# Attention and channel mix on one core: from the ninth head on, ScalarE writes the negated row maxima as diagonal blocks

## The chip, the core and the metric

The kernel runs on one core of a Trainium2 chip. Such a core has a matrix engine (TensorE, in the profile PE for matmuls and PEld for weight loads), VectorE (DVE), ScalarE (ACT), GpSimd (POOL), a queue engine that issues transfers (SyncE, SP) and 16 DMA engines. The metric is the device time of one execution in microseconds (us), as the median of several runs. A profiled execution gives the trace from which all durations below are read.

## The reference

Eight batches of eight heads: the queries are averaged in pairs (1152 to 576 rows per head), then softmax attention over 1152 keys, then a channel mix over the 512 joined features.

```python
def _attn_ref(q, k, v):
    q_pool = q.reshape(B, H, S // 2, 2, D).mean(axis=3)
    scores = scale * np.matmul(q_pool, k.transpose(0, 1, 3, 2))
    scores = scores - np.max(scores, axis=-1, keepdims=True)
    attn = np.exp(scores)
    attn = attn / (np.sum(attn, axis=-1, keepdims=True) + 1e-09)
    return np.matmul(attn, v)

def _moe_ref(x, mu_k, mu_r, w_k, w_v, w_r):
    x_prev = np.concatenate([np.zeros((B, 1, D), dtype=np.float32), x[:, :-1, :]], axis=1)
    xk = mu_k * x + (1.0 - mu_k) * x_prev
    xr = mu_r * x + (1.0 - mu_r) * x_prev
    k = np.maximum(xk @ w_k, 0.0)
    v = k * k @ w_v
    return v / (1.0 + np.exp(-(xr @ w_r)))
```

All inputs are 32-bit floats; the kernel splits each into a 16-bit high part and a 16-bit remainder and adds up the products that matter.

## The kernel before

The 64 heads are worked off one after the other, each in six blocks of 96 queries, 384 blocks in all. For one block, keys lie on the partitions: nine matmuls of 128 keys by 96 queries (line 479) put the high part of the scores into one of three PSUM buffers `s`, which rotate from block to block. The maximum over keys is found in two steps: VectorE reduces the nine chunks (line 486, tile `mx`), a matmul with the identity turns the result (line 489), VectorE reduces it to one maximum per query (line 492, tile `mb`). Then the maxima, which lie one per partition, must come to lie along a row. A matmul with `mb` as a broadcast weight and `negi`, a diagonal of -1/64, as moving operand does this (line 494, called the spread below): it leaves the negated maxima of the 96 queries on every partition of the spare columns of `s`. ScalarE copies one row of it, one partition by 96 elements, into row 96 of the low part of the transposed queries, `qT` (line 497; Prelu with two slopes makes the subtracted value a little larger than the maximum). The nine matmuls of line 503 multiply the second key operand `ks2` with that low part: rows 0 to 63 are the key's high part against the query's remainder, and row 96 of `ks2` holds 64 where the other rows from 64 on hold zero, so the same matmuls subtract the maximum. ScalarE takes the exponential (line 509), GpSimd makes its remainder (line 512), and the matmuls of lines 538, 540 and 545 multiply with the values. Every 256 rows of finished output a channel-mix tile follows (line 684, the largest part of the matmuls), whose ScalarE and VectorE work stands in lines 653 to 748.

No engine chooses its order at run time. Every operation is entered in a list with an engine, an assumed duration, the buffers it reads and writes and a due time. A planner plays the list through with these durations, tries a few orders and writes the best one out; each engine then works through its own list in that order, waiting where an operand is not there. The assumed duration of line 497 is 0.133 us. The change alters the list, so the planner makes a new order for all engines.

Of the kernel before, what the change touches and what calls it, by code (L numbers as in the profile page):

```python
# [11 lines left out]
F32 = mybir.dt.float32  # L12
F16 = mybir.dt.float16
# [3 lines left out]
AF = mybir.ActivationFunctionType  # L17
ALU = mybir.AluOpType
AX = mybir.AxisListType
PSUM = bass.MemoryType.PSUM  # L20
P = 128
# [7 lines left out]
SM = 64.0  # L29
# [8 lines left out]
EPS = 2.0 ** -10  # L38
# [4 lines left out]
O_MAX, O_EXP, O_REST, O_AV, O_EVAC, O_TURN = -6.0, 0.0, 3.0, 14.0, 6.0, 4.0  # L43
# [215 lines left out]
def kernel(  # L259
# [12 lines left out]
    nc = tc.nc  # L272
    B, H, S, D = q.shape
# [6 lines left out]
    QN = 96  # L280
# [4 lines left out]
    HALF = P // 2  # L285
    WIN = [(0, HALF, 0), (HALF, P, 1), (HALF + P, P, 3), (HALF + 2 * P, P, 4), (HALF + 3 * P, P, 5)]
    NW = len(WIN)
    TURN = [(0, 3), (3, 5)]
    assert D == 64 and DM == NG * P and TQ == NB * QN == WIN[-1][0] + P

    def spans(k0, k1):

        return WIN[k0][0], WIN[k1 - 1][0] + WIN[k1 - 1][1]

    const = ctx.enter_context(tc.tile_pool(name="const", bufs=1))
    psum = ctx.enter_context(tc.tile_pool(name="psum", bufs=1, space=PSUM))
    iss = Issue()
    op = iss.add

    def bufs(name, n, shape, dt):  # L300
        return [const.tile(shape, dt, name=f"{name}{i}") for i in range(n)]
# [8 lines left out]
    def half(x, dt, t):  # L310

        return x.bitcast(dt).rearrange("p c (q t) -> p c q t", t=2)[:, :, :, t]


    ident = const.tile([P, P], F32, name="ident")
# [2 lines left out]
    nc.gpsimd.tensor_copy(identb, ident)  # L318
    negi = const.tile([P, P], F16, name="negi")
    nc.gpsimd.tensor_scalar(negi, ident, -1.0 / SM, 1.0, op0=ALU.mult, op1=ALU.mult)  # L320


    kr, vr = bufs("kr", 2, [P, NC, D], F32), bufs("vr", 2, [P, NC, D], F32)
# [11 lines left out]
    cross = const.tile([P, D + 1], F32, name="cross")  # L335
    pl = const.tile([P, NC, TQ], F16, name="pl")
    mx, mb = bufs("mx", 3, [P, QN], F16), bufs("mb", 3, [P, 1], F16)
    den, xb = bufs("den", 2, [P, NW], F32), bufs("xb", 1, [P, NW, 2, D], F32)
    xt = bufs("xt", 3, [P, NG, TQ + 1], F32)
    xm = {n: const.tile([P, NG, T], F32, name=f"x{n}") for n in "kr"}  # L340
# [30 lines left out]

    nc.gpsimd.memset(qn[0][:, 1, :, D:P], 0.0)
    for t_ in ks2:
        nc.vector.memset(t_[D:P], 0.0)
        nc.vector.memset(t_[QN:QN + 1], SM)
    for t_ in vt:
        nc.vector.memset(t_[:, :, 2 * D:2 * D + 2], 1.0)
    for t_ in vb:
# [80 lines left out]
    def block(n, j, i, t):  # L459

        hp, z = n % 2, i % 3
        qi = n // 2 % 2
        q0 = hp * TQ + j * QN
        qhi, qlo = (qT[qi][:, r].rearrange("p j x -> p (j x)")[:, q0:q0 + QN] for r in (0, 1))
        kh, kl = ([(t_, qi, hp, j, j0) for j0, j1 in ((0, 5), (5, NQ)) if q0 < j1 * P and q0 + QN > j0 * P]
                  for t_ in ("qT", "qTl"))
        s = s_b[z]
        rows = slice(j * QN, (j + 1) * QN)
        mxz, mbz = mx[z], mb[z]

        def cols(c0, c1):
            return s[:, P + c0 * QN:P + c1 * QN]

        def grid(c0, c1):
            return cols(c0, c1).rearrange("p (c q) -> p c q", q=QN)

        def scores(c0, c1):
            for c in range(c0, c1):
                nc.tensor.matmul(cols(c, c + 1), ks1[hp][:, c, :], qhi,  # L479
                                 start=(c == c0), stop=False, skip_group_check=True)  # L480

        for c0, c1 in BK:
            op("PE", (c1 - c0) * 0.043, lambda c0=c0, c1=c1: scores(c0, c1),
               r=[("ks1", hp, c) for c in (0, 5) if c < c1 and (c0 < 5 or c)] + kh, w=[("s", z)], key=t)

        op("DVE", 0.967, lambda: nc.vector.tensor_reduce(mxz, grid(0, NC).rearrange("p c q -> p q c"),  # L486
                                                         axis=AX.X, op=ALU.max),
           r=[("s", z)], w=[("mx", z)], key=t)
        op("PE", 0.054, lambda: nc.tensor.matmul(s[0:QN, 0:P], mxz, identb, start=False, stop=False,  # L489
                                                 skip_group_check=True),  # L490
           r=[("mx", z)], w=[("s", z)], key=t + O_MAX)
        op("DVE", 0.199, lambda: nc.vector.tensor_reduce(mbz[0:QN], s[0:QN, 0:P], axis=AX.X, op=ALU.max),  # L492
           r=[("s", z)], w=[("mb", z)], key=t + O_MAX)
        op("PE", 0.05, lambda: nc.tensor.matmul(s[:, 0:QN], mbz[0:QN].broadcast_to([QN, P]),  # L494
                                                 negi[0:QN, 0:QN], start=False, stop=False, skip_group_check=True),
           r=[("mb", z)], w=[("s", z)], key=t + O_MAX)
        op("ACT", 0.133, lambda: nc.scalar.activation(qlo[QN:QN + 1], s[QN:QN + 1, 0:QN], AF.Prelu,  # L497
                                                      scale=1.0 - EPS, alpha=(1.0 + EPS) / (1.0 - EPS)),
           r=[("s", z)] + kl, w=kl, key=t + O_MAX)

        def scores2(c0, c1):
            for c in range(c0, c1):
                nc.tensor.matmul(cols(c, c + 1), ks2[hp][:, c, :], qlo,  # L503
                                 start=False, stop=True, skip_group_check=True)

        for c0, c1 in BK:
            op("PE", (c1 - c0) * 0.043, lambda c0=c0, c1=c1: scores2(c0, c1),
               r=[("ks2", hp)] + kl, w=[("s", z)], key=t + O_EXP)
        op("ACT", NC * QN / 1200 + 0.051, lambda: nc.scalar.activation(  # L509
            pf[:, :, HALF + rows.start:HALF + rows.stop], grid(0, NC), AF.Exp, bias=SHIFT, scale=0.125 / (2.0 * SQ)), r=[("s", z)], w=[("pf", j)], key=t + O_EXP)  # L510
        def lows(to, r0, r1, buf):
            op("POOL", NC * (r1 - r0) / 1000 + 0.066, lambda: nc.gpsimd.tensor_scalar(  # L512
                to, half(pf, U16, 0)[:, :, HALF + r0:HALF + r1], LO, 1.0, op0=ALU.mult, op1=ALU.mult),
               r=[("pf", j)], w=[buf], key=t + O_REST)

        r0 = rows.start
        if j == 0:
            lows(half(pf, F16, 1)[:, :, 0:HALF], 0, HALF, ("pside",))
            r0 = HALF
        lows(pl[:, :, r0:rows.stop], r0, rows.stop, ("pl", j))  # L520

    def window(n, w, t):
# [29 lines left out]
        for c0, c1 in () if side else ((0, 5), (5, NC)):  # L552
            op("PE", (c1 - c0) * 0.030, lambda c0=c0, c1=c1: lo(c0, c1),
               r=[("vb", jv)] + [("pl", j) for j in js] + [("a",)], w=[("a",)], key=t)
        if w < NW - 1:
            return

        u = a_b[:, 0:NW * VN].rearrange("p (k x) -> p k x", k=NW)
        z = n % 2
# [8 lines left out]
        op("DVE", 0.08, lambda: nc.vector.reciprocal(dz, dz), r=[("den", z)], w=[("den", z)], key=t + O_EVAC)  # L568
        op("DVE", 0.07 + NW * D / 960, lambda: nc.vector.tensor_tensor(
            xz[:, :, hh], u[:, :, 0:D], dz.unsqueeze(2).broadcast_to([P, NW, D]), op=ALU.mult),  # L570
           r=[("den", z), ("a",)], w=[("xb", hh)], key=t + O_EVAC)
        if hh == 0:
            return
        for k0, k1 in TURN:
            q0, qe = spans(k0, k1)
# [53 lines left out]
    def turn(n, m=2):  # L629
        cnt[n] += 1  # L630
        return cnt[n] % m
# [7 lines left out]
    def mix(w, t0, t1, key, dk):  # L639
# [4 lines left out]
        for c in range(NG):  # L644
            t = t0
            while t < t1:
# [3 lines left out]
                z = turn("tmp")  # L650
                xk = [("xt", b % 3, c, k0) for k0, k1 in TURN
                      if spans(k0, k1)[0] < s0 + ln and spans(k0, k1)[1] > s0 - 1]
# [112 lines left out]
    for n in range(B * H):  # L765
        b, h = divmod(n, H)
        if n and n + 1 < B * H:
            if n % 2:
                queries(n + 1, (n * NB) * PER + O_PREP - 5.0)
            prep(n + 1, (n * NB) * PER + O_PREP)  # L770
        for j in range(NB):
            i = n * NB + j
            block(n, j, i, i * PER)
            for w, (_, _, after) in enumerate(WIN):
                if after == j:
                    window(n, w, i * PER + O_AV)
        if h == H - 1:
            fkey = max(fkey, (n + 1) * NB * PER)
            while tiles and tiles[0][1] <= (b + 1) * TQ:
                fkey = ff(*tiles.pop(0), fkey, b == B - 1)  # L780
# [39 lines left out]
```

## Time and profile before

| | us |
|---|---|
| median of 3 runs | 1160.65 (1159.96 to 1161.45) |
| the profiled execution | 1158.5 |
| its span in the trace | 1156.7 |
| TensorE busy | 1105.0 (96%) |
| VectorE busy | 859.4 (74%) |
| ScalarE busy | 875.9 (76%) |
| GpSimd busy | 740.0 (64%) |

The first eight heads are blocks 1 to 48, the other 56 heads blocks 49 to 384. In the trace the 49th exponential starts at 146.3 us and the last one at 1057.5 us; what follows is the end of the channel mix. "The stage" below is 146.3 to 1057.5 us, in which the changed blocks lie. Matmuls overlap, so the duration of one is longer than the time it takes from the engine; the distance from its start to the next start is what it takes. The same is true, to a smaller degree, of ScalarE.

### The profile page before, as it was taken

To read this page: it belongs to the slowest core of one execution; us is meant where nothing else is said; L and a number is where in the kernel's file an instruction comes from. 1 tells how busy PE (TensorE), PEld (TensorE's weight loads), DVE (VectorE), ACT (ScalarE), POOL (GpSimd) and SP (SyncE) were. 2 spreads that over 40 slices of the span, in tenths; PEclk is the share of its full clock that TensorE was granted. 3 is DMA by queue.
4 is the path that set the end of the run, shared out by engine and by line. 5 is a ranking of instruction groups with operands and counts; after the bars stand their busy time and mean duration, and the time that the engine had idled before them with its cause. 6 is when DMAs were issued, how large, how long until landed. Compare 5 with 4: busy or idle time off the path is not lost.

```text
span 1156.7 us, 44885 instructions
## 1 busy us (share of the span) xinstructions
PE 1105.0 (96%) x18928; PEld 916.0 (79%) x18928; DVE 859.4 (74%) x1622; ACT 875.9 (76%) x1810; POOL 740.0 (64%) x883
## 2 busy tenths in 40 slices
PE   3878889999999999999999999999999999999998
PEld 3767787988889887978788888879797878887565
DVE  6899987888887777787687878777787778673320
ACT  4778888788778787887878786978887788775643
POOL 3767786766767567666767675857666676654431
PEclk9799999999999999999999999999999999999999
DMA  9687655466354644565444444655544444310000
GB/s 225 183 201 183 172 137 138 99 130 133 99 124 104 126 90 111 124 114 115 93 118 97 116 96 110 119 116 102 114 109 104 111 96 93 73 27 11 19 20 28
DMA packets 222378, 126.64 MB, mean 109 GB/s; under 512 B 157664, under 2 KB 194528, under 8 KB 222176
## 3 DMA queue, kind: packets, MB, share of 16 engines
q1 hardware_dynamic: 222176, 123.77, 47.1%
q8 instruction: 148, 2.42, 0.9%
q14 instruction: 54, 0.44, 0.1%
HBM read 67.11 MB, written 9.44 MB: 66 GB/s over the span
## 4 chain that ended last, share of the span: by engine, by line
PE 85%; DVE 5%; ACT 4%; DMA 3%; issue 2%; SPq 1%; ACTq 0%; DVEq 0%
PE f L684 33%; PE s L479 11%; PE s L503 11%; PE a L538 7%; PE a L540 7%; PE a L545 6%; PE s L684 4%; ACT pf L509 2%; DVE mx L486 2%; PE s L489 2%; PE a L684 2%; PE s L494 1%; PE a L581 1%; DMA ks<-kn 1%; DMA kr<-in_k_dram 1%
## 5 line engine op out<-in xcount | busy, mean ns | idle before, releaser
L486 DVE TENSOR_REDUCE mx<-s 128x96 f16<-128x864 f32 x384 | 401.5, 1054 | 107.2 <-PE s L479 59.8
L512 POOL TENSOR_SCALAR pl<-pf 128x864 f16<-128x864 uint16 (+1 forms) x384 | 337.8, 880 | 186.3 <-ACT pf L509 157.9
L509 ACT ACTIVATE pf<-s 128x864 int32<-128x864 f32 x384 | 337.6, 889 | 84.6 <-PE s L503 50.5
L479 PE MATMUL s<-qT,ks 128*128 128x96 f16 x3456 | 217.8, 208 | 25.6 <-ACT pf L509 12.7
L538 PE MATMUL a<-vt,pf 128*128 128x65 f16 x2880 | 230.2, 194 | 1.5 <-ACT pf L509 0.9
L540 PE MATMUL a<-vt,pf 128*128 128x64 f16 x2880 | 230.4, 194 | 0.0
L479 PEld LDWEIGHTS <-ks 128*128 128x128 f16 x3456 | 185.4, 99 | 51.3 <-issue 18.4
L503 PE MATMUL s<-qT,ks 128*128 128x96 f16 x3456 | 215.0, 208 | 7.5 <-ACT qT L497 6.8
L538 PEld LDWEIGHTS <-pf 128*128 128x128 f16 x2880 | 200.5, 99 | 6.3 <-ACT pf L509 1.2
L503 PEld LDWEIGHTS <-ks 128*128 128x128 f16 x3456 | 181.9, 99 | 28.7 <-issue 9.1
L540 PEld LDWEIGHTS <-pf 128*128 128x128 f16 x2880 | 192.4, 98 | 7.7 <-issue 1.0
L492 DVE TENSOR_REDUCE mb<-s 96x1 f16<-96x128 f32 x384 | 109.3, 285 | 79.9 <-PE s L489 71.8
L497 ACT ACTIVATE qT<-s 1x96 f16<-1x96 f32 x384 | 92.1, 242 | 88.4 <-PE s L494 75.7
L684 PE MATMUL f<-xhk,wk_hi 128*128 128x256 f16 x496 | 135.1, 272 | 0.2
L684 PE MATMUL f<-xlk,wk_hi 128*128 128x256 f16 x496 | 135.1, 272 | 0.0
L684 PE MATMUL f<-xhk,wk_lo 128*128 128x256 f16 x496 | 135.1, 272 | 0.0
L545 PE MATMUL a<-vb,pl 128*128 128x65 f16 x2304 | 124.0, 194 | 0.2 <-POOL pl L512 0.2
L684 PEld LDWEIGHTS <-wk_hi 128*128 128x128 f16 x1152 | 107.0, 98 | 11.0 <-issue 0.4
L435 POOL TENSOR_TENSOR kn<-kr,kn 128x320 f16<-128x320 f32 x126 | 99.6, 802 | 17.5 <-ACT kn L430 13.5
L715 POOL TENSOR_TENSOR gl<-g 128x512 f16<-128x512 f32 x72 | 77.3, 1075 | 46.1 <-ACT g L713 43.8
L545 PEld LDWEIGHTS <-pl 128*128 128x128 f16 x2304 | 99.2, 98 | 5.1 <-POOL pl L512 0.5
L489 PE MATMUL s<-identb,mx 128*96 128x128 f16 x384 | 87.6, 228 | 6.8 <-DVE mx L486 6.7
(96 smaller groups left out, 2089.9 us busy)
## 6 DMA issues: line engine op xcount, KB each, us to landing
kr<-in_k_dram SPq DMA_DIRECT2D x64, 288.0 KB, 3.0
vr<-in_v_dram SPq DMA_DIRECT2D x64, 288.0 KB, 3.2
qr<-in_q_dram SPq DMA_DIRECT2D x32, 320.0 KB, 3.4
ks<-ks SPq DMA_DIRECT2D x64, 144.0 KB, 2.5
out_dram<-em SPq DMA_DIRECT2D x36, 256.0 KB, 2.4
qr<-in_q_dram SPq DMA_DIRECT2D x32, 256.0 KB, 3.3
st<-in_moe_w_k_dram SPq DMA_DIRECT2D x8, 512.0 KB, 4.9
st<-in_moe_w_v_dram SPq DMA_DIRECT2D x8, 512.0 KB, 4.6
```

The source lines that it names most:

```text
L435: lambda cs=cs, en=nc.vector if ve else nc.gpsimd: en.tensor_tensor(kn[i][:, cs, D:P], kr[i][:, cs], kn[i][:, cs, 0:D], op=ALU.subtract),
L479: nc.tensor.matmul(cols(c, c + 1), ks1[hp][:, c, :], qhi, start=(c == c0), stop=False, skip_group_check=True)
L486: op("DVE", 0.967, lambda: nc.vector.tensor_reduce(mxz, grid(0, NC).rearrange("p c q -> p q c"), axis=AX.X, op=ALU.max), r=[("s", z)], w=[ ...
L489: op("PE", 0.054, lambda: nc.tensor.matmul(s[0:QN, 0:P], mxz, identb, start=False, stop=False, skip_group_check=True), r=[("mx", z)], w=[( ...
L492: op("DVE", 0.199, lambda: nc.vector.tensor_reduce(mbz[0:QN], s[0:QN, 0:P], axis=AX.X, op=ALU.max), r=[("s", z)], w=[("mb", z)], key=t + O ...
L503: nc.tensor.matmul(cols(c, c + 1), ks2[hp][:, c, :], qlo, start=False, stop=True, skip_group_check=True)
L509: op("ACT", NC * QN / 1200 + 0.051, lambda: nc.scalar.activation(pf[:, :, HALF + rows.start:HALF + rows.stop], grid(0, NC), AF.Exp, bias=S ...
L512: op("POOL", NC * (r1 - r0) / 1000 + 0.066, lambda: nc.gpsimd.tensor_scalar(to, half(pf, U16, 0)[:, :, HALF + r0:HALF + r1], LO, 1.0, op0= ...
L538: nc.tensor.matmul(a_b[:, a0:a0 + VN], half(pf, F16, 1)[:, c, his], vt[jv][:, c, D:D + VN], start=(w == 0 and c == 0), stop=False, skip_gr ...
L540: nc.tensor.matmul(a_b[:, a0:a0 + D], half(pf, F16, 1)[:, c, his], vt[jv][:, c, 0:D], start=False, stop=(side and c == NC - 1), skip_group ...
L545: nc.tensor.matmul(a_b[:, a0:a0 + VN], pl[:, c, rows], vb[jv][:, c, 0:VN], start=False, stop=(c == NC - 1), skip_group_check=True)
L684: nc.tensor.matmul(ps, terms[i][0], terms[i][1], start=(first and i == 0), stop=(i == last), skip_group_check=True)
```

## The change

For heads 1 to 8 everything stays. From the ninth head on (`n >= DIAG`) the second VectorE reduction writes its maxima as 32-bit floats into a new tile `mf`, and the spread is gone. In its place two ScalarE instructions read a constant diagonal `negd` (its entries are -(1 - EPS)/64) with the maxima as a scale per partition, and write the products as a 64 by 64 block and a 32 by 32 block into rows 64 to 127 and 64 to 95 of the low part of `qT`: query c has its value in row 64 + c for the first 64 queries and in row c for the other 32. All rows from 64 on of `ks2` now hold 64 instead of row 96 alone, so the matmuls of the second scores sum over the diagonal. Their number and shape are the same. The planner is told 0.233 and 0.207 us for the two instructions.

```diff
+    DIAG = H
...
+    negd = const.tile([P, P], F16, name="negd")
+    nc.gpsimd.tensor_scalar(negd, ident, -(1.0 - EPS) / SM, 1.0, op0=ALU.mult, op1=ALU.mult)
...
+    mf = bufs("mf", 3, [P, 1], F32)
...
     for t_ in ks2:
-        nc.vector.memset(t_[D:P], 0.0)
-        nc.vector.memset(t_[QN:QN + 1], SM)
+        nc.vector.memset(t_[D:P], SM)
...
-        op("DVE", 0.199, lambda: nc.vector.tensor_reduce(mbz[0:QN], s[0:QN, 0:P], axis=AX.X, op=ALU.max),
+        mo = mf[z] if n >= DIAG else mbz
+        op("DVE", 0.199, lambda: nc.vector.tensor_reduce(mo[0:QN], s[0:QN, 0:P], axis=AX.X, op=ALU.max),
            r=[("s", z)], w=[("mb", z)], key=t + O_MAX)
-        op("PE", 0.05, lambda: nc.tensor.matmul(s[:, 0:QN], mbz[0:QN].broadcast_to([QN, P]),
-                                                 negi[0:QN, 0:QN], start=False, stop=False, skip_group_check=True),
-           r=[("mb", z)], w=[("s", z)], key=t + O_MAX)
-        op("ACT", 0.133, lambda: nc.scalar.activation(qlo[QN:QN + 1], s[QN:QN + 1, 0:QN], AF.Prelu,
-                                                      scale=1.0 - EPS, alpha=(1.0 + EPS) / (1.0 - EPS)),
-           r=[("s", z)] + kl, w=kl, key=t + O_MAX)
+        tilt = (1.0 + EPS) / (1.0 - EPS)
+        if n < DIAG:
...
+        else:
+            for r0, r1 in ((0, D), (D, QN)):
+                to = qlo[D:D + r1 - r0, r0:r1]
+                op("ACT", 0.18 + (r1 - r0) / 1200, lambda to=to, r0=r0, r1=r1: nc.scalar.activation(
+                    to, negd[r0:r1, r0:r1], AF.Prelu, scale=mf[z][r0:r1], alpha=tilt),
+                   r=[("mb", z)] + kl, w=kl, key=t + O_MAX)
```

How the order moves is seen at block 159 (the third block of head 27). On TensorE before, the spread of that block (line 494) stands between value matmuls and the channel mix; `f` is the channel mix's PSUM tile, `a` that of the values:

```order
L538 MATMUL a_132<-vt1_86,pf_91 128x65
L540 LDWEIGHTS pf_91
L540 MATMUL a_132<-vt1_86,pf_91 128x64
L494 LDWEIGHTS mb2_99
L494 MATMUL s2_131<-negi_68,mb2_99 128x96
L684 LDWEIGHTS g32_111
L684 MATMUL f_133<-wv_hi_125,g32_111 128x512
```

With the change, TensorE goes from the channel mix straight to the second scores of the same block (line 515, before 503):

```order
L696 LDWEIGHTS g32_116
L696 MATMUL f_138<-wv_lo_131,g32_116 128x512
L696 LDWEIGHTS gl_117
L696 MATMUL f_138<-wv_hi_130,gl_117 128x512
L515 LDWEIGHTS ks2_0_83
L515 MATMUL s2_136<-qT1_86,ks2_0_83 128x96
```

A weight load and a matmul are gone per block; the second scores now wait for ScalarE's two writes instead of one.

On ScalarE before, around the same block, the row copies (line 497) stand singly between full-width instructions (509 the exponential, 397 the query copy):

```order
L653 ACTIVATE tmp0_115<-xt2_105,omu_r_152 128x256
L509 ACTIVATE pf_91<-s0_129 128x9x96
L497 ACTIVATE qT1_84<-s1_130 1x96
L397 ACTIVATE qn0_78<-qs0_75 128x640
L497 ACTIVATE qT1_84<-s2_131 1x96
L509 ACTIVATE pf_91<-s1_130 128x9x96
L397 ACTIVATE qn0_78<-qs0_75 128x512
L509 ACTIVATE pf_91<-s2_131 128x9x96
```

With the change, from the same exponential (line 521, before 509) on; line 509 is now the diagonal write, 400 the query copy, 433 the key copy:

```order
L521 ACTIVATE pf_93<-s0_134 128x9x96
L449 ACTIVATE vt0_87<-vr1_75 128x4x64
L509 ACTIVATE qT1_86<-negd_70,mf1_103 64x64
L433 CAST kn1_79<-kr1_73 128x4x64
L509 ACTIVATE qT1_86<-negd_70,mf1_103 32x32
L665 ACTIVATE tmp0_120<-xt2_110,omu_r_155 128x256
L521 ACTIVATE pf_93<-s1_135 128x9x96
L509 ACTIVATE qT1_86<-negd_70,mf2_104 64x64
L400 ACTIVATE qn0_80<-qs0_77 128x640
L509 ACTIVATE qT1_86<-negd_70,mf2_104 32x32
L509 ACTIVATE qT1_86<-negd_70,mf0_102 64x64
L400 ACTIVATE qn0_80<-qs0_77 128x512
```

The two halves of one block's diagonal are often put apart, with other work between them: of the 672 new instructions, 165 follow directly on another new one and 507 on a full-width or other instruction. Of the 384 row copies before, 37 follow directly on another.

More of the change, by code (lines that the diff above doesn't have):

```diff
@@ L491, in block @@
            r=[("mx", z)], w=[("s", z)], key=t + O_MAX)
-        op("DVE", 0.199, lambda: nc.vector.tensor_reduce(mbz[0:QN], s[0:QN, 0:P], axis=AX.X, op=ALU.max),
+        mo = mf[z] if n >= DIAG else mbz
+        op("DVE", 0.199, lambda: nc.vector.tensor_reduce(mo[0:QN], s[0:QN, 0:P], axis=AX.X, op=ALU.max),
            r=[("s", z)], w=[("mb", z)], key=t + O_MAX)
-        op("PE", 0.05, lambda: nc.tensor.matmul(s[:, 0:QN], mbz[0:QN].broadcast_to([QN, P]),
-                                                 negi[0:QN, 0:QN], start=False, stop=False, skip_group_check=True),
-           r=[("mb", z)], w=[("s", z)], key=t + O_MAX)
-        op("ACT", 0.133, lambda: nc.scalar.activation(qlo[QN:QN + 1], s[QN:QN + 1, 0:QN], AF.Prelu,
-                                                      scale=1.0 - EPS, alpha=(1.0 + EPS) / (1.0 - EPS)),
-           r=[("s", z)] + kl, w=kl, key=t + O_MAX)
+        tilt = (1.0 + EPS) / (1.0 - EPS)
+        if n < DIAG:
+            op("PE", 0.05, lambda: nc.tensor.matmul(s[:, 0:QN], mbz[0:QN].broadcast_to([QN, P]),
+                                                     negi[0:QN, 0:QN], start=False, stop=False, skip_group_check=True),
+               r=[("mb", z)], w=[("s", z)], key=t + O_MAX)
+            op("ACT", 0.133, lambda: nc.scalar.activation(qlo[QN:QN + 1], s[QN:QN + 1, 0:QN], AF.Prelu,
+                                                          scale=1.0 - EPS, alpha=tilt),
+               r=[("s", z)] + kl, w=kl, key=t + O_MAX)
+        else:
[4 more added lines that the diff above has]
+                   r=[("mb", z)] + kl, w=kl, key=t + O_MAX)
         def scores2(c0, c1):
```

## The prediction

> **What bounds the kernel now.** I read three views in this order: the busy times by stretch, with cuts where the 49th and the last exponential start; the waits inside the middle stretch; the time line of single instructions. In the first, a row is a stretch with the busy time and the instruction count of each engine.
>
> ```profile
> core 0: us, PE busy (x) PEld busy (x) DVE busy (x) ACT busy (x) POOL busy (x), PEclk, DMA share, GB/s
> 0.00:146.30 146.30, 105.24 (x2024) 94.24 (x2025) 125.07 (x246) 104.18 (x212) 95.61 (x118) 0.91 0.78 194
> 146.30:1057.50 911.20, 904.46 (x16230) 762.72 (x16230) 711.51 (x1332) 726.29 (x1506) 615.65 (x731) 1.00 0.48 105
> 1057.50:1156.70 99.20, 95.31 (x680) 59.06 (x676) 22.84 (x45) 45.44 (x94) 28.77 (x35) 1.00 0.06 22
> ```
>
> Only the middle row, the stage of the changed blocks, is touched. There TensorE is busy for 904.46 of 911.20 us at a granted clock of 1.00: it is the bound. ScalarE is busy for 726.29 us (80%) and idle for 184.9. The waits of TensorE in the same stage show how little it waits, and for whom (total, times, longest):
>
> ```profile
> PE s L479 <- ACT pf L509: 2.2, 5, 0.8
> PE s L494 <- DVE mb L492: 1.1, 3, 0.5
> PE s L503 <- ACT qT L497: 0.9, 2, 0.7
> ```
>
> ScalarE's waits in the stage are for TensorE:
>
> ```profile
> ACT qT L497 <- PE s L494: 63.4, 94, 2.5
> ACT pf L509 <- PE s L503: 43.2, 70, 1.6
> ACT pf L509 <- PE s L489: 13.8, 15, 1.3
> ACT r L711 <- PE f L684: 11.2, 20, 1.6
> ```
>
> So 911.2 / 336 = 2.71 us is what a block costs, all of it TensorE's, and ScalarE has 184.9 / 336 = 0.55 us per block to spare. The question is whether what is put on ScalarE fits into that.
>
> **What is removed from TensorE.** 336 spreads with their weight loads. What one takes is the distance from its start to the next start:
>
> ```profile
> 501.73 0.21 PE L494 MATMUL s<-negi,mb 96*128 96x96 f16 x1
> 501.78 0.19 PE L538 MATMUL a<-vt,pf 128*128 128x65 f16 x1
> ...
> 504.27 0.21 PE L494 MATMUL s<-negi,mb 96*128 96x96 f16 x1
> 504.31 0.19 PE L538 MATMUL a<-vt,pf 128*128 128x65 f16 x1
> ```
>
> 0.05 and 0.04 us, not the 0.21 of its duration. 336 x 0.045 = 15.1 us; with the 1.1 us of waits ahead of it, at most 336 x 0.05 + 1.1 = 17.9; at least 336 x 0.04 = 13.4. I take 15. VectorE's reduction keeps its size and writes four bytes for two into 96 partitions: nothing. The memory fills of `ks2` and the building of `negd` lie at the start, once: nothing. The second scores keep 9 matmuls of 96 columns whatever is in the rows: nothing. No transfer is added.
>
> **What is added to ScalarE.** The groups of the stage (line, shape, count | busy us, mean ns of one) that carry the price:
>
> ```profile
> L509 ACT ACTIVATE pf<-s 128x864 int32<-128x864 f32 x336 | 295.6, 889 | 74.2 <-PE s L503 43.2 <-PE s L489 13.8 <-PE a L540 6.4
> L497 ACT ACTIVATE qT<-s 1x96 f16<-1x96 f32 x334 | 80.3, 242 | 73.4 <-PE s L494 63.4 <-DVE ex L739 1.2 <-DVE mx L486 1.2
> L446 ACT ACTIVATE vt<-vr 128x256 f16<-128x256 f32 x54 | 22.1, 410 | 0.5
> L653 ACT ACTIVATE tmp<-xt,omu_r 128x256 f32<-128x256 f32 x39 | 19.4, 506 | 0.9 <-DVE xr L656 0.4
> L562 ACT ACTIVATE cross<-a 64x65 f32<-64x65 f32 x55 | 12.0, 218 | 2.2 <-PE a L545 0.6
> L653 ACT ACTIVATE tmp<-xt,omu_r 128x128 f32<-128x128 f32 x16 | 6.2, 395 | 0.3 <-DVE xr L656 0.3
> L653 ACT ACTIVATE tmp<-xt,omu_r 128x64 f32<-128x64 f32 x12 | 4.1, 345 | 1.3 <-DVE xr L656 1.1
> ```
>
> The new instructions read the on-chip memory, write it, and take their scale from a tile, as line 653 does. At 64 columns that row has 345 ns. From 64 to 128 columns it grows by 50 ns, 0.8 ns a column, so 32 columns take 345 - 26 = 319. That a scale from a tile costs is seen at 256 columns: 506 ns (L653) against 410 (L446, a constant scale). Sum of the two: 0.664 us per block, in place of one row copy of 0.242. Busy time: 336 x 0.422 = +142 us.
>
> That is not all, and here I read the time line of ScalarE (start, duration):
>
> ```profile
> 505.42 0.47 ACT L446 ACTIVATE vt<-vr 128x320 f16<-128x320 f32 x1
> 505.92 0.22 ACT L562 ACTIVATE cross<-a 64x65 f32<-64x65 f32 x1
> 506.16 0.42 ACT L446 ACTIVATE vt<-vr 128x256 f16<-128x256 f32 x1
> 506.49 0.72 ACT L397 ACTIVATE qn<-qs 128x640 f16<-128x640 f32 x1
> 507.23 0.24 ACT L497 ACTIVATE qT<-s 1x96 f16<-1x96 f32 x1
> 507.50 0.89 ACT L509 ACTIVATE pf<-s 128x864 int32<-128x864 f32 x1
> 508.29 0.62 ACT L397 ACTIVATE qn<-qs 128x512 f16<-128x512 f32 x1
> 508.80 0.88 ACT L509 ACTIVATE pf<-s 128x864 int32<-128x864 f32 x1
> ```
>
> Between two instructions on all 128 partitions the second starts before the first ends: 507.50 + 0.89 is 508.39, the next start 508.29, an overlap of 0.10 (0.11 at 508.80, 0.09 at 506.49). Next to one on fewer partitions, 64 in L562 and 1 in L497, there is none, before or behind it, but a gap of 0.02 to 0.03 on either side. All 119 row copies that directly follow an exponential behave so in the trace. The new instructions write 64 and 32 partitions, starting at the same partition 64 as L562 does, so I take them to lose the overlap too. Each run of such instructions then costs its neighbour's overlap and two gaps, some 0.155 us. In the order there are 308 runs of row copies in the stage before and 507 runs of new ones: 199 x 0.155 = 31 us, and 165 x 0.03 = 5 us for gaps inside runs. Added in all: 142 + 31 + 5 = 178 us.
>
> The page "ScalarE: Activation LUTs" of the Trainium skill (section "What ACT_TABLE_LOAD costs") speaks against this price: an activation takes 186 ns plus 0.833 ns a column, 93 more per operand pointer, and back-to-back ones overlap by about 93. By it the pair would take 0.33 + 0.31 - 0.19 = 0.45 us, an estimate, in which the planner's own figures nearly agree. The durations of L653 agree with it; the overlap next to partial widths does not. What would follow if it held here is the first rival.
>
> **Does it fit?** ScalarE's own need in the stage before: at most its 726 us busy plus the gaps, 363 runs (308 and 55 of L562) x 0.05 = 18, so 744. At least 705, if for every start in the stage the shortest usual distance of its kind to the next start is added up over all 1506 (exponential 0.77, row copy 0.27 and so on): the rest of the busy time is overlap that was lost because the next instruction was still waiting. With 178 more the need is 883 to 922, middle 902. TensorE's need is 904 - 15 = 889, or 896 with the 7 us it now idles. So both engines would be full, each in an order fixed by a planner that counted 0.44 us per block for what takes some 0.9 with the lost overlaps. The 185 us of slack are used up by 178.
>
> Two full engines that feed each other don't stay full. What is queued behind a late diagonal on ScalarE is the exponential of the block before or after (65 of 336 pairs have one between their halves, 0.89 us), which frees a score buffer for line 479; and the second scores stand in TensorE's queue ahead of everything else. From the end of VectorE's reduction to the second scores it was a matmul of 0.21 and a copy of 0.24; it is 0.69 at least. So TensorE will wait for ScalarE at L479 and L515. How much idle time ScalarE keeps when it is the fullest engine no row tells directly. TensorE, as the bound, kept 0.7% (6.7 of 911). The other end is VectorE early in the run:
>
> ```profile
> 50.00:100.00 50.00, 39.58 (x855) 36.05 (x853) 45.00 (x87) 40.04 (x82) 35.21 (x41) 0.93 0.79 184
> 100.00:200.00 100.00, 89.00 (x1623) 74.81 (x1620) 89.23 (x170) 82.54 (x171) 74.55 (x88) 0.98 0.60 151
> ```
>
> It was the fullest engine from 50 to 200 us and still idled 15.8 of 150 (10.5%), with DMA at 0.60 to 0.79 beside it, more than in the stage. I take 4%, below the middle of 0.7 and 10.5 for that reason. Stage: 902 / 0.96 = 940 us, 28 more than 911. The profiled execution of 1158.5 becomes 1187; it stands 2.15 below the median, so **1189 us** against 1160.65.
>
> Its own range: need 883 with 0.7% idle gives 889, where TensorE's 896 takes over (-15, rival B); need 922 with 7% idle gives 991 (+80, 1241). Between the likelier ends, 883 at 3% (910, no change) and 922 at 6% (981, +70), it is 1161 to 1231.
>
> **Rivals.** A: the overlap holds for the new instructions, since the order of writes or the start partition and not the width decides it. Then the pair costs 0.664 - 0.20 = 0.46 and replaces 0.242 + 0.155 = 0.40; ScalarE's need grows by 336 x 0.06 = 20, to 725 to 764, TensorE stays the bound and the 15 us are won: 1146. Against it are the L562 rows, which have the same width and the same target partition; for it, that no row has a scale from a tile at this width. 0.16.
>
> B: the overlap is lost, but ScalarE packs tightly. Its 185 us of idle time were waits for a TensorE that was the bound; where it is late itself, its operands are there. Need 883 at under 1% idle, TensorE 896: 896 to 905, -6 to -15, about 1150. It needs the least price and a well-fitting order. 0.11.
>
> C, slower still: both engines interlock as VectorE and TensorE did from 50 to 200 us. 902 / 0.895 = 1008, +97, about 1257; it decides once ScalarE is late at most blocks, since each wait of TensorE delays the next maximum. 0.09.
>
> D: price and gain cancel within 0.2%, 2.3 us, which is about what can be told from no change here: 0.04.
>
> **How the numbers follow.** Forecast 0.60, A 0.16, B 0.11, C 0.09, D 0.04. Faster is A, nearly all of B: 0.26. Same is D and the edge of B: 0.05. Slower is the forecast and C: 0.69. The range takes in B, most of A and the forecast's ends, and leaves out most of C and A's lower half: 1146 to 1234.
>
> **What would show it.** Right: the new instructions at some 345 and 319 ns and each neighbour starting 0.02 to 0.03 after the end; ScalarE busy by some 868 us in the stage of 940 (726 + 142, and lost overlaps of about 20 more that count as busy), TensorE busy under 97%, with waits at L479 and L515 for ScalarE above 30 us where they were 2.2 and 0.9. Wrong: TensorE still over 99% busy in the stage (A or B; an overlap of 0.1 next to the new instructions tells A), or the time lost to VectorE, whose row has 200 us of idle time and should only follow.

## The result and the profile after

The changed kernel takes 1191.53 us (median of 4 runs, 1189.0 to 1192.77) against 1160.31 before (now four runs): ratio 1.0269, 95% interval 1.0245 to 1.0293. It is slower. 1189 was predicted.

The busy times by stretch of the kernel after, cut again at the 49th and the last exponential:

```profile
core 0: us, PE busy (x) PEld busy (x) DVE busy (x) ACT busy (x) POOL busy (x), PEclk, DMA share, GB/s
0.00:149.30 149.30, 106.77 (x2022) 96.82 (x2023) 125.56 (x243) 104.78 (x213) 96.37 (x119) 0.86 0.75 191
149.30:1088.40 939.10, 912.63 (x15897) 755.77 (x15897) 700.99 (x1333) 866.12 (x1841) 604.16 (x730) 1.00 0.46 102
1088.40:1187.20 98.80, 94.94 (x677) 58.64 (x673) 23.96 (x45) 46.02 (x94) 28.66 (x35) 1.00 0.06 22
```

The stage grew from 911.2 to 939.1 us, the part before it from 146.3 to 149.3, the end is the same. ScalarE's busy time in the stage went from 726.3 to 866.1, while TensorE lost 333 matmuls of its 16230 and is still "busy" longer: a matmul is recorded with 0.2 us where the next one can start 0.04 after it, and what is recorded past that point counts as busy although TensorE waits. The two writes, from the groups of the whole run:

```profile
L509 ACT ACTIVATE qT<-negd,mf 64x64 f16<-64x64 f16 x336 | 115.1, 346 | 19.9 <-DVE mf L496 11.2 <-DVE a L576 0.9
L509 ACT ACTIVATE qT<-negd,mf 32x32 f16<-32x32 f16 x336 | 104.4, 314 | 6.6
```

346 and 314 ns each. ScalarE's longest waits in the stage, and TensorE's (total, times, longest):

```profile
ACT pf L521 <- PE s L515: 11.8, 25, 1.6
ACT qT L509 <- DVE mf L496: 11.2, 23, 1.2
...
PE s L482 <- ACT pf L521: 12.0, 29, 1.6
PE s L515 <- ACT qT L509: 4.9, 17, 0.6
```

ScalarE's waits for TensorE, 63.4 and 43.2 us before, have shrunk to a fraction, and TensorE now waits for ScalarE. The wait list understates this. Adding up, over all matmuls of the stage, by how much the distance to the next start exceeds the usual one of its shape (the 20th percentile), gives 34 us before and 76 after; of the 76, 47 lie ahead of score matmuls (L482, L515), where it was 10 before (L479, L503). At usual distances TensorE's work went from 877 to 862. So -15 for the work and +42 for waiting make up 27 of the stage's 28.

TensorE's granted clock explains little of this: it is 1.00 in the stage's row before and after. Cut finer, it is 0.97 from 149.3 to 285.0 us of the kernel after and 1.00 behind that, which is worth 4 us at most (an estimate, 3% of 135.7).

ScalarE's time line shows the lost overlap (start, duration):

```profile
523.56 0.32 ACT L509 ACTIVATE qT<-negd,mf 32x32 f16<-32x32 f16 x1
523.90 0.63 ACT L749 ACTIVATE em<-em 128x512 f32<-128x512 f32 x1
524.55 0.22 ACT L574 ACTIVATE cross<-a 64x65 f32<-64x65 f32 x1
524.67 0.33 ACT L509 ACTIVATE qT<-negd,mf 64x64 f16<-64x64 f16 x1
525.03 0.89 ACT L521 ACTIVATE pf<-s 128x864 int32<-128x864 f32 x1
```

Behind the 32 by 32 write the next starts 0.02 us after its end, and so on down the rows, with one exception: the 64 by 64 write at 524.67 starts 0.10 before L574 ends. Both write 64 partitions from partition 64 on. The experiments come back to this exception.

### The profile page after: what moved, and what is told of

It reads as the page before. It is cut to its first block, busy times and chain, and to the rows that moved or that the text cites. A ratio compares the mean times of both kernels' runs of the same rounds, so it can differ in the third digit from the quotient of the medians.

```text
span 1187.2 us, 44299 instructions
## 1 busy us (share of the span) xinstructions
PE 1114.3 (94%) x18592; PEld 911.2 (77%) x18592; DVE 850.5 (72%) x1620; ACT 1016.9 (86%) x2146; POOL 729.2 (61%) x884
## 4 chain that ended last, share of the span: by engine, by line
PE 57%; ACT 28%; DVE 5%; issue 5%; DMA 2%; POOL 1%; SPq 0%; ACTq 0%; DVEq 0%; POOLq 0%
PE f L696 21%; ACT pf L521 9%; PE s L515 8%; PE s L482 8%; ACT qT L509 7%; PE a L550 5%; PE a L552 5%; PE s L696 4%; PE a L557 4%; DVE mx L489 2%; PE a L696 2%; ACT vt L449 2%; ACT kn L433 1%; ACT tmp L665 1%; PE s L492 1%
## 5 line engine op out<-in xcount | busy, mean ns | idle before, releaser
L524 POOL TENSOR_SCALAR pl<-pf 128x864 f16<-128x864 uint16 (+1 forms) x384 | 333.9, 870 | 214.0 <-ACT pf L521 188.7
L482 PE MATMUL s<-qT,ks 128*128 128x96 f16 x3456 | 219.5, 209 | 31.9 <-ACT pf L521 16.2
L509 ACT ACTIVATE qT<-negd,mf 32x32 f16<-32x32 f16 (+1 forms) x672 | 219.5, 330 | 26.5 <-DVE mf L496 11.2
L482 PEld LDWEIGHTS <-ks 128*128 128x128 f16 x3456 | 187.8, 100 | 63.1 <-issue 29.7
L515 PE MATMUL s<-qT,ks 128*128 128x96 f16 x3456 | 218.6, 210 | 16.8 <-ACT qT L503 7.8
L515 PEld LDWEIGHTS <-ks 128*128 128x128 f16 x3456 | 187.6, 100 | 49.9 <-issue 27.9
L496 DVE TENSOR_REDUCE mf<-s 96x1 f32<-96x128 f32 x336 | 94.2, 282 | 75.6 <-PE s L492 72.8
```

What stands on the lines that cost most here:

```text
L482: nc.tensor.matmul(cols(c, c + 1), ks1[hp][:, c, :], qhi, start=(c == c0), stop=False, skip_group_check=True)
L509: op("ACT", 0.18 + (r1 - r0) / 1200, lambda to=to, r0=r0, r1=r1: nc.scalar.activation(to, negd[r0:r1, r0:r1], AF.Prelu, scale=mf[z][r0:r1] ...
L515: nc.tensor.matmul(cols(c, c + 1), ks2[hp][:, c, :], qlo, start=False, stop=True, skip_group_check=True)
```

## The experiments

Theory: ScalarE is filled by the two writes, by their duration and by the overlap lost around them, and TensorE and ScalarE then hold each other up. Rivals: it is the order made from wrong durations; it is the longer chain from the maximum to the second scores; the overlap has another cause or plays no part.

**One block left out.**

```diff
-            for r0, r1 in ((0, D), (D, QN)):
+            for r0, r1 in ((0, D),):
```

> The 32 by 32 write is left out, so the last 32 queries of each block from the ninth head on keep their maximum unsubtracted; everything else is as in the changed kernel. Theory (ScalarE is the full engine): its need in the stage falls by 336 x (0.314 + 0.03) plus some 250 lost overlaps of 0.13, about 148 us, from 893 to 745, below TensorE's 896; TensorE bounds again without the spread, 1145 to 1150. Rival (not ScalarE's time, but the longer chain from the maximum to the second scores, or the new order): one write still stands in that chain, 1165 to 1190.

Measured 1148.51 us, ratio 0.9901 (0.9884 to 0.9919).

```profile
146.70:1047.70 901.00, 890.85 (x15889) 750.25 (x15889) 716.53 (x1342) 754.12 (x1509) 612.93 (x732) 1.00 0.49 107
```

As the theory expected. With ScalarE's busy time down by 112 us the stage takes 901, 10 less than before the change. A diagonal write in the chain and the missing spread are still there, so neither is the loss. The chain is one write shorter than the changed kernel's; the wide kernel below, which keeps both writes, rules that out too.

**The planner told the longer durations.**

```diff
-                op("ACT", 0.18 + (r1 - r0) / 1200, ...
+                op("ACT", 0.42 + (r1 - r0) / 1200, ...
```

> Only the planner's durations are changed: 0.473 and 0.447 us for the two writes instead of 0.233 and 0.207, about what they take with the lost overlaps. Theory: the work is the same and fills ScalarE in any order; a better fit wins a part of its 47 us of waits, 1172 to 1190. Rival (the wrong figures made a bad order, and that is the loss): 1165 or less.

Measured 1187.21 us, ratio 1.0242 (1.0222 to 1.0262), within the theory's range.

```profile
145.90:1086.90 941.00, 906.57 (x15906) 754.34 (x15904) 690.18 (x1323) 865.86 (x1827) 607.13 (x726) 1.00 0.46 102
```

The order is another, the stage's loss the same. The planner's wrong figures are not the cause.

**The spread kept.**

```diff
         else:
+            op("PE", 0.05, lambda: nc.tensor.matmul(s[:, 0:QN], mbz[0:QN].broadcast_to([QN, P]),
+                                                     negi[0:QN, 0:QN], start=False, stop=False, skip_group_check=True),
+               r=[("mb", z)], w=[("s", z)], key=t + O_MAX)
             for r0, r1 in ((0, D), (D, QN)):
```

> The changed kernel with the spread matmul put back in its place on TensorE (its result, made from old maxima, is not read). Theory: TensorE has time to spare, so its 15 us come almost for nothing, 1191 to 1198. Rival (both engines are equally full, and TensorE's time still counts in full): 1206 or more.

Measured 1196.14 us, ratio 1.0317 (1.0296 to 1.0339): 4.6 more than the changed kernel, as the theory had it. But the row of the stage says something else:

```profile
143.90:1094.20 950.30, 924.36 (x16237) 769.39 (x16237) 705.75 (x1338) 873.20 (x1845) 607.06 (x733) 1.00 0.45 102
```

The stage is 11.2 us longer than the changed kernel's 939.1; the part before it, which has no changed work, happened to be 5.4 shorter (143.9 against 149.3). By the distances of starts, TensorE's work is 15 us more than in the changed kernel (877 against 862) and its waiting 4 less (72 against 76), so some 11 of the 15 us count. TensorE had hardly any time to spare: both engines seem to set the pace together, and the theory that ScalarE alone does is too simple. The order is a new one here too, so the 11 may hold a part of that.

**Every second block.**

```diff
+        dg = n >= DIAG and i % 2 == 1
-        mo = mf[z] if n >= DIAG else mbz
+        mo = mf[z] if dg else mbz
...
-        if n < DIAG:
+        if not dg:
```

> Only every second block from the ninth head on writes diagonals, the others keep the spread and the row copy. Theory (a threshold: nothing is lost until ScalarE is full): ScalarE's need grows by 89 instead of 178, to some 800 to 830 of 903, TensorE saves 7.5 us: 1151 to 1158, faster than before. Rival (each diagonal costs its own delay in the chain): half of the loss, about 1176.

Measured 1161.97 us, ratio 1.0022 (1.0007 to 1.0036); both expectations missed.

```profile
140.90:1060.90 920.00, 907.16 (x16078) 761.47 (x16078) 710.87 (x1343) 804.61 (x1681) 608.15 (x736) 0.99 0.47 105
```

The stage is 8.8 us longer than before the change, which a first part that came out 5.4 us shorter hides in the total. ScalarE is busy for only 87% of it; 93 us are waits (gaps over 0.04 us). TensorE's time above the usual distances is 50 us here, against 34 before and 76 with all blocks. In this order, then, waiting sets in before ScalarE is full. But the order, in which row copies and diagonals alternate, may be the reason: the kernels below that keep ScalarE busy for 91 or 92% of the stage have only 40 to 41 us of such time. That is not settled.

**Wide against narrow.** Two kernels with the same list of operations, and so the same order (in the traces the four compute engines have the same instructions in the same order); a scratch tile `dg` of 128 rows is the moving operand of the second scores from the ninth head on. They differ in the partitions of the two writes alone, from the narrow to the wide:

```diff
-                    dg[z][D:D + r1 - r0, r0:r1], negd[r0:r1, r0:r1], AF.Prelu, scale=mf[z][r0:r1], alpha=tilt),
+                    dg[z][:, r0:r1], negd[:, r0:r1], AF.Prelu, scale=mf[z], alpha=tilt),
```

> From the ninth head on the two writes go to a scratch tile of 128 rows, all 128 partitions at once (128 by 64 and 128 by 32), and the second scores take that tile as moving operand in place of the low part of the queries, so the remainder term is left out and the subtracted values are not the maxima. Number, order, columns and waits of the instructions are those of the next kernel; only the partitions differ. Theory (narrow width costs the overlap): the pair takes 0.66 - 0.2 instead of 0.66 + 0.2, the need of ScalarE falls by some 100 us or more, 1146 to 1160. Rival (the scale from a tile, or Prelu, costs the overlap, or it is no matter of overlap at all): as the next kernel, 1185 to 1195.

> The same scratch tile as moving operand (the remainder term is left out), but with the writes of the changed kernel, 64 and 32 partitions from partition 64 on. Both theories: as the changed kernel, 1185 to 1195.

Wide: 1143.72 us, ratio 0.9871 (0.9847 to 0.9896). Narrow: 1189.15, ratio 1.0258 (1.0237 to 1.0278). The wide one is 2 us below the theory's range. The stage, one group and a piece of the time line of the wide one, then the same of the narrow one:

```profile
151.10:1046.60 895.50, 888.19 (x15898) 749.93 (x15899) 710.83 (x1337) 776.38 (x1841) 610.84 (x731) 1.00 0.48 107
L511 ACT ACTIVATE dg<-negd,mf 128x64 f16<-128x64 f16 x336 | 114.7, 344 | 25.2 <-DVE mf L499 19.8 <-DVE den L582 3.4 <-DVE den L580 0.4
```

```profile
504.06 0.62 ACT L748 ACTIVATE em<-f 128x512 f32<-128x512 f32 x1
504.54 0.37 ACT L511 ACTIVATE dg<-negd,mf 128x64 f16<-128x64 f16 x1
504.77 0.65 ACT L750 ACTIVATE ex<-ex 128x512 f32<-128x512 f32 x1
```

```profile
149.40:1089.50 940.10, 912.40 (x15898) 755.58 (x15899) 700.14 (x1335) 865.56 (x1841) 603.15 (x732) 1.00 0.46 102
L511 ACT ACTIVATE dg<-negd,mf 64x64 f16<-64x64 f16 x336 | 115.1, 346 | 19.7 <-DVE mf L499 10.0 <-DVE den L582 1.5 <-DVE den L580 0.3
```

```profile
504.60 0.35 ACT L511 ACTIVATE dg<-negd,mf 64x64 f16<-64x64 f16 x1
504.97 0.46 ACT L436 CAST kn<-kr 128x320 f16<-128x320 f32 x1
```

The durations are equal (344 and 346 ns). Only the overlap differs: in the wide one the write starts 0.14 before its neighbour ends and the next 0.14 before the write does; in the narrow one the next starts 0.02 behind it. That is worth 45 us of the program. Added up over the stage, ScalarE's overlaps come to 144 us in the wide kernel and 56 in the narrow one. This is rival A's condition, made true: with writes that overlap, and the same number and shape of matmuls, the kernel is 15 us faster than before the change. (It leaves out the query's remainder.)

**VectorE writes the diagonals.**

```diff
-                op("ACT", 0.18 + (r1 - r0) / 1200, ... nc.scalar.activation(
-                    to, negd[r0:r1, r0:r1], AF.Prelu, scale=mf[z][r0:r1], alpha=tilt),
...
+                op("DVE", 0.09 + (r1 - r0) / 960, ... nc.vector.tensor_scalar(
+                    to, negd[r0:r1, r0:r1], mf[z][r0:r1], 1.0, op0=ALU.mult, op1=ALU.mult),
```

> VectorE writes the two diagonal blocks instead of ScalarE (one slope for both signs of the maximum, which the softmax does not see). Theory: ScalarE loses the row copy and what it costs, some 126 us, and is far from full; VectorE gets 336 x 0.28 = 94 us or so on top of 711, 805 of 896; TensorE bounds: 1143 to 1152, faster than before. Rival (VectorE becomes the next full engine, or waits for the memory port that it shares with GpSimd): 1160 to 1185.

Measured 1277.11 us, ratio 1.1016 (1.0966 to 1.1065): slower, as the rival had it, but far above its range too. One of VectorE's groups, and pieces of its time line and of GpSimd's:

```profile
L509 DVE TENSOR_SCALAR qT<-negd,mf 64x64 f16<-64x64 f16 x336 | 110.8, 344 | 8.8
```

```profile
505.13 0.23 DVE L509 TENSOR_SCALAR qT<-negd,mf 64x64 f16<-64x64 f16 x1
510.98 0.80 DVE L509 TENSOR_SCALAR qT<-negd,mf 64x64 f16<-64x64 f16 x1
510.95 1.43 POOL L438 TENSOR_TENSOR kn<-kr,kn 128x320 f16<-128x320 f32 x2
```

The same write takes 0.23 us at 505.13 and 0.80 at 510.98, where a GpSimd instruction had just begun. Of the 336 of this size, the 200 with no GpSimd instruction beside them take 236 ns at most; the others up to 1112. All 81 that take more than 250 ns end 0.03 to 0.04 us after a GpSimd instruction has ended. VectorE is busy for 921 of the stage's 1026 us. The page "SBUF — State Buffer" of the Trainium skill (section "SBUF: two separate sides") names a lock on a pair of ports that VectorE, in some of its instructions, and GpSimd share: the one that starts first has it for its whole instruction. The ends in this trace agree.

**All of the reference with wide writes, from the ninth head on and from the first.** The diagonal comes with the transposed query remainder, ScalarE scales it in place on 128 partitions, and VectorE's second reduction is split in two to bring the maxima to partition 64.

```diff
+                op("DVE", 0.199, ... nc.vector.tensor_reduce(mo[D:D + r1 - r0], s[r0:r1, 0:P], axis=AX.X, op=ALU.max),
...
+                op("ACT", 0.18 + (r1 - r0) / 1200, ... nc.scalar.activation(
+                    qlo[:, r0:r1], qlo[:, r0:r1], AF.Copy, scale=mo),
```

> A version that computes all of the reference with wide writes. The constant diagonal is put into the columns 64 to 127 of the query remainder ahead of its transposition, so it arrives in rows 64 to 127 of the low part of the transposed queries by the transfer that runs anyway; ScalarE then multiplies the whole 128 by 64 and 128 by 32 columns in place with a scale per partition, 1 in the first 64 rows and the maxima in the others. For that VectorE reduces the turned maxima in two instructions, to two tiles, in place of one. From the ninth head on. Theory: ScalarE as in the kernel with wide scratch writes, not full; VectorE gets 336 x 0.2 = 67 us more, 778 of 896; TensorE bounds without the spread: 1143 to 1152. Rival (VectorE's second reduction makes the maximum late, or fills VectorE locally): 1158 to 1175.

> The same from the first head on; the spread is gone everywhere. The first eight heads are the part of the run in which VectorE is fullest (10% idle), so the second reduction costs there about 48 x 0.2 = 10 us while TensorE's 2 us are worth nothing. Theory: 2 to 10 us more than the version from the ninth head on. Rival (VectorE's idle time there takes it in): the same or 2 us less.

From the ninth head on 1195.16 us, ratio 1.0308 (1.0287 to 1.033), above both expectations; from the first 1202.3, ratio 1.0376 (1.0352 to 1.0401), 7 us more. ScalarE is relieved as meant (busy for 784 of 945 us), but VectorE is now busy for 91% of the stage. The row of the stage, from the ninth head on, and VectorE's time line:

```profile
149.60:1095.10 945.50, 909.80 (x15902) 751.94 (x15901) 859.78 (x1666) 784.22 (x1840) 604.13 (x732) 1.00 0.45 102
```

```profile
501.25 0.28 DVE L509 TENSOR_REDUCE ma<-s 64x1 f32<-64x128 f32 x1
501.56 0.29 DVE L509 TENSOR_REDUCE mc<-s 32x1 f32<-32x128 f32 x1
501.88 1.06 DVE L498 TENSOR_REDUCE mx<-s 128x96 f16<-128x864 f32 x1
```

There is 0.03 us of gap behind each: VectorE loses its overlap too. Before, its one reduction of 96 partitions from 0 on started ahead of its predecessor's end 193 times of 384 and was overlapped by its successor 230 times. The expected 67 us became 148 of busy time: 97 by the durations of the reductions (192.3 us for the two, against 336 x 0.285), 20 by overlap that is gone, the rest by other VectorE instructions that took longer; why they did was not looked into. It was this trace that spoke against the number of partitions as the cause.

The 7 us more of the version from the first head on lie in the expected range, but not for the expected reason alone, as its stretches show:

```profile
0.00:167.00 167.00, 112.13 (x1980) 100.98 (x1981) 146.98 (x290) 113.32 (x257) 95.74 (x126) 0.80 0.65 164
167.00:1102.70 935.70, 904.92 (x15927) 754.29 (x15924) 844.57 (x1676) 789.40 (x1849) 608.85 (x734) 0.99 0.46 104
```

The first eight heads take 17.4 us more (167.0 against 149.6), where some 10 were expected, and the unchanged rest 9.8 less.

**Narrow writes to partition 0.**

```diff
-                    dg[z][D:D + r1 - r0, r0:r1], negd[r0:r1, r0:r1], ...
+                    dg[z][0:r1 - r0, r0:r1], negd[r0:r1, r0:r1], ...
```

> As the kernel with narrow writes to a scratch tile (the remainder term is left out), but the two blocks are written to partitions 0 to 63 and 0 to 31 of it in place of 64 to 127 and 64 to 95; the values that are subtracted are not the maxima. Theory S (the overlap is lost because the writes don't start at partition 0; VectorE's reduction to 96 partitions from 0 on does overlap with its neighbours): as the wide one, 1143 to 1152. Theory N (it is lost because of the number of partitions): as the narrow one, 1187 to 1192.

Measured 1152.82 us, ratio 0.9952 (0.9937 to 0.9968): at the edge of theory S.

```profile
149.00:1052.10 903.10, 892.75 (x15898) 751.29 (x15899) 703.00 (x1336) 820.05 (x1841) 611.04 (x732) 1.00 0.48 106
```

How often neighbours overlap in the traces, in three kernels whose ScalarE order is alike (in the wide one, nearly all of the rest waited):

| first, then next | changed (to 64) | wide | narrow, to 0 |
|---|---|---|---|
| other full-width, then the 64-wide | 0 of 266 | 217 of 266 | 198 of 266 |
| the 64-wide, then full-width | 1 of 215 | 196 of 215 | 207 of 215 |
| full-width, then the 32-wide | 0 of 208 | 208 of 208 | 0 of 208 |
| the 32-wide, then full-width | 0 of 264 | 196 of 264 | 75 of 264 |

The 64-wide write, which now reads and writes from partition 0 on, overlaps like one on all 128. The 32-wide one still reads from partition 64 and mostly doesn't; its 75 overlaps are all with successors that read PSUM, the memory that matmuls write (75 of the 78 that did not wait), none with one of the 142 that read the on-chip memory (SBUF) and did not wait. So it is the partition at which reading and writing start, not their number, and reading counts by memory. Put as a rule: an instruction starts ahead of its predecessor's end when it starts to read at the partition at which the last instruction on that same memory started to read, and to write at that of the last write there. Applied to all ScalarE instructions of the 14 traces of this case, the rule says "no overlap" for 11461 of them, and none overlaps; of the 14229 others that did not wait (started at most 0.045 us behind the end), 13799 overlap. It also takes in the exception above: L574 reads PSUM and writes from partition 64, so the 64 by 64 write behind it finds the last write at 64 and the last read of the on-chip memory at 0, where its own are.

**The layout swapped.** All of the reference, with the remainder in rows 64 to 127 and the diagonals in rows 0 to 63.

```diff
-        nc.vector.memset(t_[D:P], SM)
+        nc.vector.memset(t_[0:D], SM)
...
-                qn[0][:, 1, js, 0:D], qs[0][:, js], SQ, ...
+                qn[0][:, 1, js, D:P], qs[0][:, js], SQ, ...
...
-        op("DMA", 0.47, lambda: nc.sync.dma_start(ks2[i][0:D], ks1[i][0:D]),
+        op("DMA", 0.47, lambda: nc.sync.dma_start(ks2[i][D:P], ks1[i][0:D]),
...
-                to = qlo[D:D + r1 - r0, r0:r1]
+                to = qlo[0:r1 - r0, r0:r1]
```

> A version that computes all of the reference with the layout turned round: the query remainder lies in rows 64 to 127 of the low part, the key's high part is copied to the same rows of the second key operand, and rows 0 to 63 take the 64 and the diagonal blocks (for the first eight heads the row copy, in row 0). Nothing else differs from the changed kernel. Theory S: the writes overlap again and ScalarE isn't full, 1143 to 1152, faster than both. Theory N: as the changed kernel, 1187 to 1194.

> The swapped layout again, with only the planner's durations changed: 0.24 us for the 64-wide write, which overlaps, and 0.42 for the 32-wide one, which does not. Theory: ScalarE is no longer full, so the order matters little: 1152 to 1157, the same as the swapped layout within its measurement. Rival (the stage still loses to waits for ScalarE that a truer order removes): 1145 to 1151.

Swapped: 1155.27 us, ratio 0.9974 (0.9964 to 0.9984). With the truer durations: 1147.62, ratio 0.9886 (0.9862 to 0.9909). Both take less than the kernel before, by 0.3% and 1.1%, and the second is the fastest version here that computes all of the reference. The time line of the first of the two, its stretches, and those of the second:

```profile
502.81 0.89 ACT L521 ACTIVATE pf<-s 128x864 int32<-128x864 f32 x1
503.58 0.34 ACT L509 ACTIVATE qT<-negd,mf 64x64 f16<-64x64 f16 x1
503.82 0.62 ACT L725 ACTIVATE g<-r 128x512 f32<-128x512 f32 x1
504.47 0.32 ACT L509 ACTIVATE qT<-negd,mf 32x32 f16<-32x32 f16 x1
504.81 0.42 ACT L449 ACTIVATE vt<-vr 128x256 f16<-128x256 f32 x1
```

```profile
0.00:153.30 153.30, 107.91 (x2022) 97.86 (x2023) 126.20 (x243) 103.71 (x213) 96.53 (x119) 0.87 0.75 186
153.30:1055.50 902.20, 891.92 (x15897) 750.83 (x15897) 704.68 (x1333) 820.21 (x1841) 609.41 (x730) 1.00 0.48 106
```

```profile
0.00:143.00 143.00, 105.91 (x2021) 96.16 (x2021) 121.47 (x237) 101.11 (x210) 92.69 (x118) 0.87 0.80 193
143.00:1047.00 904.00, 892.65 (x15925) 750.96 (x15926) 707.56 (x1339) 831.40 (x1846) 616.81 (x732) 1.00 0.49 107
```

The 64-wide write overlaps on both sides (0.12 and 0.10), the 32-wide on neither. The first kernel lies 3 us above theory S's range: its stage is 9.0 us shorter than before the change, its first eight heads 7.0 longer. Between the two kernels the stage is the same (902.2 and 904.0), as the theory says; the 8 us lie in the first eight heads (153.3 and 143.0), in which the changed line does not even occur. So they come from another order there, not from a better fit around the diagonals, and the rival's number came true for a reason of which it did not speak.

## Why the prediction was right

- **TensorE's saving, 15 us:** confirmed. At usual distances its work in the stage fell by 15 (877 to 862).
- **The price of the writes, 345 and 319 ns, +142 us busy:** measured 346 and 314; ScalarE's busy time in the stage is 866 where 868 was forecast. The 20 more for lost overlaps that count as busy did not show.
- **The lost overlap, 36 us:** there, and the cause of the loss, as the wide and the narrow kernel show, which differ in nothing else and by 45 us in time. As a term of the sum it was too large. ScalarE's need (the stage less its gaps over 0.04 us) went from 741.1 to 892.6, by 151.5; the durations make up 136 of it, which leaves 15. The overlaps sum to 58 us before and 56 after, since the writes broke some, but 332 starts had waited before (more than 0.04 us behind the end) and only 110 do now. Against writes that do overlap the price is far higher: the wide kernel's need is 780. The page's rule of 93 ns for back-to-back activations ("ScalarE: Activation LUTs" of the Trainium skill, section "What ACT_TABLE_LOAD costs") holds where both start at the same partitions (median overlap 97 ns between full-width ones in the changed kernel), and not elsewhere; by it alone the result would have been rival A.
- **The reason given for it failed.** The step "Next to one on fewer partitions [...] there is none" named the number of partitions. The runs showed the start partition in its place: 64 partitions from 0 on overlap. The rows used (L562, L497) both write from elsewhere than partition 0, and next to full-width ones could not tell the two apart. The trace before could have: VectorE's 96 partitions from 0 on overlap, and so do row copies with each other. Of the 119 row copies behind an exponential, none overlaps with that, but 7 with what follows, 5 of these with another row copy. Two such copies of one partition each, at 0.24 us a copy, take 0.38 together:

```profile
406.88 0.38 ACT L497 ACTIVATE qT<-s 1x96 f16<-1x96 f32 x2
```

- **902 us of need at 4% idle, 940 us:** the need measured is 893, and the 46.5 us of gaps over 0.04 are 4.9% of the stage's 939.1. A need 9 us too large and an idle share too small cancelled, and the 902 itself was the sum of a start taken too low (the middle of 705 and 744; measured 741) and an addition too high (178; measured 151.5). The 4% was a choice between 0.7 and 10.5, not a reading. That 1189 came within 3 us is luck of these sizes, while the mechanism was the one forecast.
- **Nothing outside the stage:** 3.0 us were lost in the first eight heads. Over the kernels here that part took 141 to 167 us; leaving out the one with changed work in it, 141 to 154. It moves from kernel to kernel. TensorE's granted clock was lower there as well (0.86 against 0.91 before); whether that or the order cost the 3.0 us is not shown.
- **What would show it:** TensorE's busy share is 97.2%, not under 97, and the listed waits at L482 and L515 sum to 17 us, not over 30. The mechanism is there (47 us by the distances of starts), but these two views hide it, since a matmul's recorded end, which is modelled, covers the first 0.17 us or so of every wait.
- **Two full engines that feed each other:** supported by the spread that counted for some 11 of 15 when put back, in one new order. That nothing is lost as long as ScalarE is not full is not borne out by the kernel with every second block (50 us of waiting against 34), but its order may be the reason.

## What to carry to other kernels

Price an added instruction by the distance between starts, next to neighbours like the ones it will have, not by a formula from other rows; the start partitions of what it reads and writes, and those of the instructions around it, belong to its price. Before moving work off a full engine, add up what the receiver has left: 185 us of idle time did not hold 151.5 of added need, because the idle time was waiting that the two engines did for each other. And where a planner remakes the whole order, compare stage by stage: between two kernels that differ in the planner's figures alone, a part whose work did not change moved by 10 us.

## What the runs showed of the hardware

- A ScalarE instruction overlaps by about 0.09 to 0.10 us (median 0.098) with the one before it where it reads from the partition at which the last read of the same memory started, and writes from that of the last write (13799 of 14229 that did not wait, in 14 traces); where one of the two differs, there is no overlap (none of 11461) and the usual gap is 0.025. The number of partitions does not matter: instructions on 1, 32 and 64 partitions behind one on as many overlap too where the rule lets them (52 of 53, 100 of 100 and 214 of 219). On-chip memory and PSUM count apart, so an instruction that reads PSUM can overlap behind one that reads the on-chip memory from another partition (75 of 78 behind the 32-wide write). The starts that occur here are 0, 64 and 96.
- VectorE behaves alike as far as seen: in nearly all cases two reductions to partition 64 had 0.03 us of gap or more on both sides (10 of 672 started ahead of the end before them), where one from 0 on started ahead in 193 of 384.
- A 64 by 64 VectorE multiplication in 16 bits took 0.23 us alone and up to 1.11 us when a GpSimd instruction was running, and then ended 0.03 to 0.04 us after that one.
